# A decode step of attention and MLP: VectorE's keys in two steps of 24 blocks instead of four of 12

## The chip, the cores and the metric

One core of a Trainium2 chip runs the whole program. The metric is the device time of one execution in microseconds (us). A core has five engines that run their own instruction streams and meet only through semaphores: TensorE (PE, matmuls and transposes), VectorE (DVE), ScalarE (ACT), GpSimd (POOL) and SyncE (SP), which here issues nearly all DMAs. Data moves between device memory and the on-chip memory by DMA engines, and matmul results land in a second on-chip memory, PSUM.

## The reference

For one token `x` (512 values) the program computes two branches and mixes them by a gate. Branch A is attention over a cache of 4096 keys and values for each of 32 heads of 128 dimensions; branch B is an MLP with a squared ReLU.

```python
x = A_x
g = sigmoid((x * gate_w).sum(-1))
# A
q = (x @ wq)                                   # 32 heads x 128
scores = einsum("bhqd,bhkd->bhqk", q, k_cache) * 128 ** -0.5
o = einsum("bhqk,bhkd->bhqd", softmax(scores), v_cache)
a = o.reshape(1, 1, 4096) @ wo                 # 4096 -> 512
# B
h = x @ w1 + b1                                # 512 -> 1376
b = relu(h) ** 2 @ w2 + b2                     # 1376 -> 512
out = g * a + (1 - g) * b
```

The caches are 32 x 4096 x 128 in bf16, 33.6 MB each; with the weights 78.47 MB are read.

## The kernel before, in words

**Quads.** The heads are worked four at a time: a quad `q` (0 to 7) is four heads. A quad's keys are one load of 4 MiB (K0 to K7): partition `32 r + p` holds head `r`'s keys `128 p` to `128 p + 127`, one behind the other. The 128 keys of a partition are called blocks: block `b` is one key of each partition, 128 elements wide. Values are loaded likewise (V0 to V7; V7 in three parts). Two buffers are there for keys and two for values, so K of quad `q` can be loaded only when quad `q - 2` no longer needs its buffer.

**Scores on two engines.** The 128 blocks are shared out. 48 of them (`X_BLOCKS`, four runs of 12) go to VectorE: `ttr(q, j)` multiplies 12 blocks of keys by the query (`qb`, spread over the partitions) into `prod`, fp32 (L685), and sums each block's 128 products into one column of `S` (L689). The other 80 (`Y_BLOCKS`) go to TensorE, in ten groups of eight: `transposes` (L460), ScalarE copies them from PSUM (`evac`, L355), `scores` multiplies them by the query (L467), and ScalarE copies the result to `S` (`s_copy`, L361). `COLUMN` gives the column of `S` that a block has.

**Softmax and values.** VectorE's `smax(q)` takes the maximum of each partition (L694). TensorE turns the column of maxima into a row (`max_rows`, L488), VectorE takes the maximum of each head (`gmax`, L698 and L701), TensorE spreads it (`max_cols`, L492), and ScalarE computes the exponentials and their sums (`exps`, L372). `pv(q)` on TensorE sums the denominators (L497) and multiplies by the values (128 matmuls, L501). VectorE's `recip(q)` and `norm(q)` divide and multiply by the gate (L708, L716); `norm` signals `s_on`.

**Output.** For two quads at a time TensorE turns the normed outputs (`turn`, L519), spreads them (`spread`, L525) and multiplies by a quarter of `wo` (`out_rows`, L534; the loads are wo0 to wo3). The MLP's first layer (`mlp_h`, L509 and L513) runs once near the end, and the second (`mlp_out`, L545) last of all, from `w2a` (ten groups of 128 rows) and `w2b` (the 96 rows left over), loaded in five parts.

**TensorE's order** is a loop of turns written with branches; turn `t` works quads `2t` and `2t + 1`. In block `h1`, from turn 2 on, it takes one `s_on` and then runs `pv` of an odd quad; `turn` takes another `s_on`. Each taking waits for one `norm`, so the eight `norm` are taken in their order: `norm(0)` ahead of `pv(1)`, `norm(1)` in the next `turn`, `norm(2)` ahead of `pv(3)`, `norm(3)` in `turn`, `norm(4)` ahead of `pv(5)`, `norm(5)` in `turn`, `norm(6)` ahead of `pv(7)`, `norm(7)` in the last `turn`. Around them the order is: in turn 3 `pv(3)`, `max_rows(5)`, keys of quad 6, `max_cols(5)`, `turn`, `spread`, `pv(4)`, `out_rows`, `max_rows(6)`, keys of quad 7, `max_cols(6)`; in turn 4 `pv(5)`, `max_rows(7)`, `max_cols(7)`, `turn`, `spread`, `mlp_h`, `pv(6)`, `out_rows`; then `pv(7)`, `turn`, `spread`, `out_rows` and `mlp_out`.

**VectorE's order** is the loop at L733: for each quad four `ttr`, with small work in between: behind the first one `bias()` (in quad 1), behind the second `gmax` of the quad before, behind the third `recip` and `norm` of the quad three before (from quad 3 on), and `smax` at the end.

**SyncE's order** is `ORDER`: K0 K1 V0 K2 K3 V1 K4 V2 K5 V3 K6 V4 K7 V5 V6 V7, each load from quad 2 on behind a wait (`done`): for keys that VectorE (`s_sd`, L246) and TensorE's transposes (`s_t`, L247) are through with quad `q - 2`, for values that `pv(q - 2)` is (`s_pv`, L249). `w1` goes behind V0, wo0 behind K2, wo1 behind V4 and wo2 behind V5 (`WO_AT`), and wo3 and the parts of `w2` come at the end, the latter behind a wait for VectorE's last `ttr` (L275), since `prod` lies in the memory of `w2a` (L102). All go into one queue.

Of the kernel before, what the change touches and what calls it, by code (L numbers as in the profile page):

```python
# [5 lines left out]
def bass_gated_mix__gqa_block_cached__dense_activation_squared_relu__decode_kernel(  # L6
# [15 lines left out]
    fp32 = mybir.dt.float32  # L22
    bf16 = mybir.dt.bfloat16
# [6 lines left out]
    DM = 512  # L30
    F = 1376
    FG = 10
    FR = F - FG * 128
# [4 lines left out]
    R = 4  # L38
    NQ = NH // R
    NB = 128  # L40
    NP = 4
    PB = NB // NP
    XB = 12
    YB = PB - XB
    YQ = NP * YB
    GB = 8
    GQ = YQ // GB
    NS = 4
# [15 lines left out]
    QF = 4  # L64
    W2_PARTS = [(0, 4), (4, 8), (FG, FG + 1), (8, 9), (9, 10)]


    X_BLOCKS = [PB * j + b for j in range(NP) for b in range(XB)]
    Y_BLOCKS = [PB * j + b for j in range(NP) for b in range(XB, PB)]
    COLUMN = {b: c for c, b in enumerate(Y_BLOCKS + X_BLOCKS)}  # L70

    k_q = A_k_cache.rearrange("a (q r) (p b) d -> (a q) (r p) (b d)", r=R, p=32)
# [7 lines left out]
    with ctx:  # L80
        def sb(name, shape, dt):
            return ctx.enter_context(nc.sbuf_tensor(name, shape, dt))
# [4 lines left out]
        def sem(name):  # L87
            return ctx.enter_context(nc.semaphore(name))

        KV = sb("KV", [128, 4, NB * 128], bf16)  # L90
        W = sb("W", [128, 4 * 4096], bf16)
# [5 lines left out]
        sel0 = W[0:GH, 2 * TB * DM:2 * TB * DM + 2048]  # L97
        selB = sel0.rearrange("h (a c p) -> h a c p", a=2, c=8)
        w1_sb = sb("w1_sb", [128, 4, F], bf16)
        w2a = sb("w2a", [128, FG, DM], bf16)  # L100

        prod = w2a[:, :, :].rearrange("p g n -> p (g n)").bitcast(fp32)[:, 0:XB * 128]\  # L102
            .rearrange("p (b d) -> p b d", d=128)
        w2b = sb("w2b", [FR, DM], bf16)
        xcol = sb("xcol", [128, 4], bf16)
        xcolf = sb("xcolf", [128, 4], fp32)
        xrow = w1_sb[0:1, 0, 0:DM]
# [12 lines left out]
        qc2 = sb("qc2", [128, 2, R], bf16)  # L120
        S = sb("S", [128, NS, NB], fp32)
        E = sb("E", [128, 2, NB, R], bf16)
        mp = sb("mp", [128, 2], fp32)
# [69 lines left out]
        s_sd = sem("s_sd")  # L193
        s_pd = sem("s_pd")
# [23 lines left out]
        def key(q, b):  # L218
            return KV[:, K_SLOT[q], b * 128:(b + 1) * 128]

        def rows(r):
            return slice(32 * r, 32 * r + 32)
# [6 lines left out]
        @block.sync  # L229
        def _(eng):  # L230
            def load_kv(n):
                kind, q = ORDER[n]
                if q >= 2:
                    done(kind, q - 2)
                if kind == "K":
                    eng.dma_start(KV[:, K_SLOT[q], :], k_q[q, :, :]).then_inc(s_k[q], 16)
                else:
                    at = 0
                    for m, sv in zip(V_PARTS[q], s_v[q]):
                        a, b = at * PB * 128, (at + m) * PB * 128  # L240
                        eng.dma_start(KV[:, V_SLOT[q], a:b], v_q[q, :, a:b]).then_inc(sv, 16)  # L241
                        at += m

            def done(kind, q):
                if kind == "K":
                    eng.wait_ge(s_sd, NP * (q + 1))  # L246
                    eng.wait_ge(s_t, GQ * (q + 1))  # L247
                else:
                    eng.wait_ge(s_pv, q + 1)  # L249

            def load_wo(g):
                if g == 0:
                    eng.wait_ge(s_qps, NQ)
                elif g < NG - 1:
                    eng.wait_ge(s_wd, g)
                a = 0 if g < NG - 1 else 1
                eng.dma_start(wo_sb[:, a, :, :], wo_v[g, :, :, :]).then_inc(s_wo[a], 16)  # L257

            def load_w2(n):
                a, b = W2_PARTS[n]  # L260
                if a < FG:
                    eng.dma_start(w2a[:, a:b, :], w2_v[:, a:b, :]).then_inc(s_w2[n], 16)  # L262
                else:
                    eng.dma_start(w2b[:, :], B_w2[FG * 128:F, :]).then_inc(s_w2[n], 16)  # L264

            for n in range(len(ORDER)):
                load_kv(n)
                if n == 2:
                    eng.wait_ge(s_z, 1)
                    eng.wait_ge(s_b2, 1)  # L270
                    eng.dma_start(w1_sb[:, :, :], w1_v[:, :, :]).then_inc(s_w1, 16)
                if n in WO_AT:
                    load_wo(WO_AT[n])
            load_wo(NG - 1)
            eng.wait_ge(s_sd, NP * NQ)  # L275
            load_w2(0)
            load_w2(1)
            load_w2(2)
            load_w2(3)
            load_w2(4)  # L280
            eng.wait_ge(s_f4, 1)
            eng.dma_start(out[0, 0, :].rearrange("(j p) -> j p", p=128), fin4[:, :]).then_inc(s_out, 16)
# [38 lines left out]
        def _(eng):  # L321
# [35 lines left out]
            def s_copy(q):  # L357
                eng.wait_ge(s_s2, GQ * (q + 1))
                S2 = pS[:, 0:YQ * R].rearrange("p (b r) -> p b r", r=R)
                for r in range(R):  # L360
                    eng.activation(S[rows(r), q % NS, 0:YQ], S2[rows(r), :, r], ACT.Copy).then_inc(s_cp, 1)  # L361

# [45 lines left out]
        def _(eng):  # L408
# [48 lines left out]
            def transposes(a, g):  # L457
                for y in range(GB):
                    b = Y_BLOCKS[GB * g + y]
                    mm = eng.transpose(KP[(GQ * a + g) % NKP][:, y * 128:(y + 1) * 128], key(a, b), ident[:, :])  # L460
# [34 lines left out]
            def pv(a):  # L495
                take(s_e, R)
                eng.matmul(DEN[a], onesf[:, :], RS[:, a, :], start=True, stop=True)  # L497
                for j in range(NP):
                    take(s_vp)
                    for b in range(PB * j, PB * j + PB):  # L500
                        mm = eng.matmul(O[a], KV[:, V_SLOT[a], b * 128:(b + 1) * 128],  # L501
                                        E[:, a, COLUMN[b], :], start=(b == 0), stop=(b == NB - 1))
                mm.then_inc(s_pv, 1)
# [146 lines left out]
        def _(eng):  # L650
# [20 lines left out]
            def bias():  # L671
                eng.wait_ge(s_b2, 1)
                eng.tensor_scalar(b2g[:, :], B2, omg[:, 0:1], None, ALU.mult).then_inc(s_bg, 1)

            def ttr(q, j):
                if j == 0:
                    eng.wait_ge(s_k[q], 16)
                    eng.wait_ge(s_qb, R * (q + 1))
                    if q >= NS:
                        eng.wait_ge(s_pv, q - NS + 1)  # L680
                if q + j > 0:
                    eng.wait_ge(s_sd, NP * q + j)
                x = PB * j * 128
                c = COLUMN[PB * j]
                eng.tensor_tensor(prod, KV[:, K_SLOT[q], x:x + XB * 128].rearrange("p (b d) -> p b d", d=128),  # L685
                                  qb[:, q, :].unsqueeze(1).to_broadcast([128, XB, 128]), ALU.mult)\
                   .then_inc(s_pd, 1)
                eng.wait_ge(s_pd, NP * q + j + 1)
                eng.tensor_reduce(S[:, q % NS, c:c + XB], prod, AX.X, ALU.add).then_inc(s_sd, 1)  # L689

            def smax(q):
                eng.wait_ge(s_cp, R * (q + 1))
                eng.wait_ge(s_sd, NP * (q + 1))
                eng.tensor_reduce(mp[:, q % 2:q % 2 + 1], S[:, q % NS, :], AX.X, ALU.max).then_inc(s_mp, 1)  # L694

            def gmax(q):
                eng.wait_ge(s_mt, q + 1)
                eng.tensor_reduce(gm[:, q, :], MT.rearrange("o (r p) -> o r p", r=R), AX.X, ALU.max)\  # L698
                   .then_inc(s_gm, 1)
                eng.wait_ge(s_gm, q + 1)  # L700
                eng.tensor_scalar(dg[:, q % 2, :].rearrange("o (r p) -> o r p", r=R),  # L701
                                  gm[:, q, :].unsqueeze(2).to_broadcast([1, R, 32]), -SCALE, None, ALU.mult)\
                   .then_inc(s_dg, 1)

            def recip(q):
                a, b = R * q, R * q + R
                eng.wait_ge(s_pv, q + 1)
                eng.reciprocal(rden[:, a:b], DEN[q % 2]).then_inc(s_rd, 1)  # L708

            def norm(q):  # L710
                a, b = R * q, R * q + R
                eng.wait_ge(s_rd, q + 1)
                if q >= 2:

                    eng.wait_ge(s_ot, q // 2 * 2 - 1)
                eng.scalar_tensor_tensor(out=onorm[:, q % 2, :], in0=O[q % 2], scalar=gcol[:, 0:1],  # L716
                                         in1=rden[:, a:b], op0=ALU.mult, op1=ALU.mult)\
                   .then_inc(s_on, 1)
# [12 lines left out]
                                         op0=ALU.mult, op1=ALU.mult).then_inc(s_hs, 1)  # L731
            gate()
            for q in range(NQ):  # L733
                for j in range(NP):
                    ttr(q, j)
                    if j == 0 and q == 1:
                        bias()
                    if j == 1 and q >= 1:
                        gmax(q - 1)
                    if j == 2 and q >= 3:  # L740
                        recip(q - 3)
                        norm(q - 3)
                smax(q)
# [46 lines left out]
```

## Time and profile before

| what | value |
|---|---|
| three runs, median | 190.8 us (190.54 to 190.84) |
| the profiled execution | 190.55 us, span 189.2 us |
| PE busy | 137.1 us (72%) |
| VectorE busy | 123.0 us (65%) in 123 instructions |
| ScalarE busy | 116.0 us (61%) |
| read from device memory | 78.32 MB, 414 GB/s over the span |
| DMA queue 1, share of 16 engines | 97.1% |
| VectorE, products (L685) | 32 of 128 x 1536, mean 1760 ns, 56.3 us |
| VectorE, sums (L689) | 32 of 128 x 1536, mean 1753 ns, 56.1 us |
| VectorE idle before L685, for keys | 19.0 us in six waits |
| mean granted TensorE clock | 0.735 |

The profile is one execution, and its span runs from the first to the last instruction; what lies around it, 190.55 less 189.2, is 1.35 us. Busy time is counted by engine; DMA issues and waits are not busy. In a timeline a line gives the start and the duration in us, the engine, the line of the kernel, the operation, what it writes and reads, and in brackets how long its engine was idle before and what ended that. "SPq" is the queue of SyncE's DMA issues, "PEq" TensorE's sequencer, and "issue" time in which no releaser is seen.

### The profile page before, as it was taken

How to read it: one execution, taken by the hardware profiler on the slowest of the kernel's cores; microseconds unless marked ns; L12 is line 12 of the kernel's file. 1: busy time of each engine (PE TensorE's matmuls, PEld its weight loads, DVE VectorE, ACT ScalarE, POOL GpSimd, SP SyncE). 2: the span in 40 equal slices, each digit the busy share in tenths (PEclk: the TensorE clock that was granted, in tenths of full speed). 3: DMA queues.
4: the chain of work that ended last, by engine and by line, in shares of the span. 5: the costliest groups of instructions: out<-in, count | busy, mean ns of one | idle time of the engine just before them, and what ended most of it. 6: DMA issues, size and time to landing. Idle time of an engine off the chain costs nothing. (4 is left out here: it accounts for less than half of the span.)

```text
span 189.2 us, 6234 instructions
## 1 busy us (share of the span) xinstructions
PE 137.1 (72%) x2688; PEld 119.8 (63%) x2688; DVE 123.0 (65%) x123; ACT 116.0 (61%) x243; POOL 6.0 (3%) x13
## 2 busy tenths in 40 slices
PE   0009297668849979969968797829868496889865
PEld 0003165537739779758958696829767495879864
DVE  0110099979969999996998299919990499701010
ACT  3004559948989986984987099708973298560000
POOL 4000000000700000000000000000000000000000
PEclk9999969958975975995795559655985579555555
DMA  6999999989989999999999999999999999999992
GB/s 225 437 444 443 443 443 426 443 361 483 440 360 436 443 443 440 417 436 430 443 424 409 423 443 443 436 436 436 414 445 409 416 443 443 438 388 416 421 388 78
DMA packets 4177, 78.47 MB, mean 415 GB/s; under 512 B 483, under 2 KB 837, under 8 KB 1094
## 3 DMA queue, kind: packets, MB, share of 16 engines
q1 hardware_dynamic: 4152, 78.32, 97.1%
q8 instruction: 7, 0.11, 0.2%
q14 instruction: 4, 0.03, 0.0%
q10 hardware_dynamic: 14, 0.01, 0.0%
HBM read 78.32 MB, written 0.00 MB: 414 GB/s over the span
## 5 line engine op out<-in xcount | busy, mean ns | idle before, releaser
L355 ACT ACTIVATE kT<-KP 128x1024 bf16<-128x1024 bf16 x80 | 75.3, 1041 | 26.1 <-PE KP L460 25.9
L685 DVE TENSOR_TENSOR w2a<-KV,qb 128x1536 f32<-128x1536 bf16 x32 | 56.3, 1760 | 19.4 <-DMA KV<-in_A_k_cache_dram 19.0
L460 PE MATMUL KP<-ident,KV 128*128 128x128 bf16 x640 | 59.6, 256 | 10.5 <-PEq L455 10.5
L460 PEld LDWEIGHTS KP<-ident,KV 128*128 128x128 bf16 x640 | 48.4, 116 | 14.1 <-issue 13.1
L689 DVE TENSOR_REDUCE S<-w2a 128x12 f32<-128x1536 f32 x32 | 56.1, 1753 | 1.1
L467 PE MATMUL pS<-qc,kT 128*128 128x4 bf16 x640 | 28.1, 166 | 13.0 <-PEq L455 11.0
L467 PEld LDWEIGHTS pS<-qc,kT 128*128 128x128 bf16 x640 | 24.6, 99 | 18.9 <-issue 17.6
L501 PEld LDWEIGHTS pO<-E,KV 128*128 128x128 bf16 x1024 | 29.3, 105 | 0.0
L501 PE MATMUL pO<-E,KV 128*128 128x4 bf16 x1024 | 28.4, 166 | 0.0
L372 ACT ACTIVATE E<-S,nM 32x128 bf16<-32x128 f32 x32 | 18.5, 578 | 0.9
L445 PE MATMUL pQ<-W,xb 128*128 128x512 bf16 x20 | 7.8, 532 | 7.2 <-DMA W<-in_A_wq_dram 6.1
L338 ACT ACTIVATE qb<-pQ 32x128 bf16<-32x128 f32 x20 | 5.4, 268 | 9.7 <-PE pQ L445 9.3
L361 ACT ACTIVATE S<-pS 32x80 f32<-32x80 f32 x32 | 7.3, 228 | 4.8 <-PE pS L467 4.2
L445 PEld LDWEIGHTS pQ<-W,xb 128*128 128x128 bf16 x20 | 2.2, 126 | 9.6 <-DMA W<-in_A_wq_dram 6.2
L372 ACT ACTIVATION_READ_ACCUMULATOR E<-S,nM 32x1 f32 x32 | 8.1, 252 | 0.0
L664 DVE TENSOR_SCALAR e<-ez 128x1 f32<-128x1 f32 x1 | 0.2, 153 | 10.8 <-ACT ez L387 10.8
L708 DVE RECIPROCAL rden<-pO 128x4 f32<-128x4 f32 x8 | 1.4, 174 | 8.2 <-PE pO L501 8.2
L594 PE MATMUL pO<-ident,w_sb 1*128 1x1 bf16 x4 | 0.3, 165 | 7.8 <-DMA w_sb<-in_A_x_dram 7.8
L497 PE MATMUL pO<-RS,onesf 128*128 128x4 f32 x16 | 4.3, 339 | 1.8 <-PEq L455 1.8
L655 DVE TENSOR_SCALAR xb<-zeros,xcolf 128x128 bf16<-128x128 bf16 x4 | 0.7, 248 | 7.5 <-ACT xcolf L331 7.5
L488 PE MATMUL pM<-identf,mp 128*1 128x128 f32 x8 | 3.0, 372 | 3.4 <-PEq L455 3.1
L497 PEld LDWEIGHTS pO<-RS,onesf 128*128 128x128 f32 x16 | 3.8, 298 | 2.1 <-issue 2.0
(75 smaller groups left out, 72.2 us busy)
## 6 DMA issues: line engine op xcount, KB each, us to landing
KV<-in_A_k_cache_dram SPq DMA_DIRECT2D x8, 4096.0 KB, 22.0
KV<-in_A_v_cache_dram SPq DMA_DIRECT2D x7, 4096.0 KB, 29.5
W<-in_A_wq_dram SPq DMA_DIRECT2D x1, 4096.0 KB, 13.4
W<-in_A_wo_dram SPq DMA_DIRECT2D x4, 1024.0 KB, 16.5
KV<-in_A_v_cache_dram SPq DMA_DIRECT2D x1, 2048.0 KB, 11.0
KV<-in_A_v_cache_dram SPq DMA_DIRECT2D x2, 1024.0 KB, 14.1
w_sb<-in_B_w_dram SPq DMA_DIRECT2D x1, 1376.0 KB, 24.4
w2a<-in_B_w_dram SPq DMA_DIRECT2D x2, 512.0 KB, 18.5
```

Of the source, the lines that this page charges most:

```text
L338: eng.activation(qb[rows(r), c, :], QR[c][rows(r), r * 128:(r + 1) * 128], ACT.Copy)\
L355: eng.activation(kT[:, n % NT, :], KP[n % NKP][:, :], ACT.Copy).then_inc(s_ev, 1)
L361: eng.activation(S[rows(r), q % NS, 0:YQ], S2[rows(r), :, r], ACT.Copy).then_inc(s_cp, 1)
L372: eng.activation(E[rows(r), q % 2, :, r], S[rows(r), q % NS, :], ACT.Exp, bias=nM[rows(r), q:q + 1], scale=SCALE, accum_out=RS[rows(r), q ...
L445: mm = eng.matmul(QR[c], xb[:, t, :], wq_sb[:, t, c * 512:(c + 1) * 512], start=(t == 0), stop=(t == 3))
L460: mm = eng.transpose(KP[(GQ * a + g) % NKP][:, y * 128:(y + 1) * 128], key(a, b), ident[:, :])
L467: mm = eng.matmul(pS[:, R * c:R * c + R], kT[:, (GQ * a + g) % NT, y * 128:(y + 1) * 128], qc2[:, a, :], start=True, stop=True)
L488: eng.transpose(MT, mp[:, a:a + 1], identf[:, :]).then_inc(s_mt, 1)
L497: eng.matmul(DEN[a], onesf[:, :], RS[:, a, :], start=True, stop=True)
L501: mm = eng.matmul(O[a], KV[:, V_SLOT[a], b * 128:(b + 1) * 128], E[:, a, COLUMN[b], :], start=(b == 0), stop=(b == NB - 1))
L685: eng.tensor_tensor(prod, KV[:, K_SLOT[q], x:x + XB * 128].rearrange("p (b d) -> p b d", d=128), qb[:, q, :].unsqueeze(1).to_broadcast([12 ...
L689: eng.tensor_reduce(S[:, q % NS, c:c + XB], prod, AX.X, ALU.add).then_inc(s_sd, 1)
```

## The change

A quad's first 48 blocks are VectorE's, in one run, instead of four runs of 12; they are worked in `NX` = 2 steps of `XB` = 24 blocks. The counts in the waits on `s_sd` and `s_pd` follow (`NX` for `NP`). `prod` grows from 12 to 24 blocks, 12 KiB a partition; it lies in a new buffer `w2x` of `FG + 2` rows of 512, of which `w2a` is the first ten and `w2b` row ten. In VectorE's loop `gmax` goes behind the first of two steps, and `recip` and `norm` behind the second.

```diff
-    XB = 12
-    YB = PB - XB
-    YQ = NP * YB
+    NX = 2
+    XB = 24
+    YQ = NB - NX * XB
...
-    X_BLOCKS = [PB * j + b for j in range(NP) for b in range(XB)]
-    Y_BLOCKS = [PB * j + b for j in range(NP) for b in range(XB, PB)]
+    X_BLOCKS = list(range(NX * XB))
+    Y_BLOCKS = list(range(NX * XB, NB))
...
-        w2a = sb("w2a", [128, FG, DM], bf16)
-        prod = w2a[:, :, :].rearrange("p g n -> p (g n)").bitcast(fp32)[:, 0:XB * 128]\
+        w2x = sb("w2x", [128, FG + 2, DM], bf16)
+        w2a = w2x[:, 0:FG, :]
+        w2b = w2x[0:FR, FG, :]
+        prod = w2x[:, :, :].rearrange("p g n -> p (g n)").bitcast(fp32)[:, 0:XB * 128]\
             .rearrange("p (b d) -> p b d", d=128)
-        w2b = sb("w2b", [FR, DM], bf16)
...
-                    eng.wait_ge(s_sd, NP * (q + 1))
+                    eng.wait_ge(s_sd, NX * (q + 1))
...
-                    eng.wait_ge(s_sd, NP * q + j)
-                x = PB * j * 128
-                c = COLUMN[PB * j]
+                    eng.wait_ge(s_sd, NX * q + j)
+                x = XB * j * 128
+                c = COLUMN[XB * j]
...
-                for j in range(NP):
+                for j in range(NX):
                     ttr(q, j)
                     if j == 0 and q == 1:
                         bias()
-                    if j == 1 and q >= 1:
+                    if j == 0 and q >= 1:
                         gmax(q - 1)
-                    if j == 2 and q >= 3:
+                    if j == 1 and q >= 3:
                         recip(q - 3)
                         norm(q - 3)
                 smax(q)
```

The waits on `s_sd` ahead of the `w2` loads, on `s_pd` in `ttr` and on `s_sd` in `smax` change from `NP` to `NX` in the same way.

More of the change, by code (lines that the diff above doesn't have):

```diff
@@ L274, in _ @@
             load_wo(NG - 1)
-            eng.wait_ge(s_sd, NP * NQ)
+            eng.wait_ge(s_sd, NX * NQ)
             load_w2(0)
@@ L687, in ttr @@
                    .then_inc(s_pd, 1)
-                eng.wait_ge(s_pd, NP * q + j + 1)
+                eng.wait_ge(s_pd, NX * q + j + 1)
                 eng.tensor_reduce(S[:, q % NS, c:c + XB], prod, AX.X, ALU.add).then_inc(s_sd, 1)
@@ L692, in smax @@
                 eng.wait_ge(s_cp, R * (q + 1))
-                eng.wait_ge(s_sd, NP * (q + 1))
+                eng.wait_ge(s_sd, NX * (q + 1))
                 eng.tensor_reduce(mp[:, q % 2:q % 2 + 1], S[:, q % NS, :], AX.X, ALU.max).then_inc(s_mp, 1)
```

## The prediction

> **What bounds the kernel now.** I read the page's slices first, then the chain of waits that ended last, then SyncE's own timeline, and last the timelines of the engines from the landing of the last keys to the end.
>
> The slices, GB/s and busy tenths of the DMA engines:
>
> ```profile
> DMA  6999999989989999999999999999999999999992
> GB/s 225 437 444 443 443 443 426 443 361 483 440 360 436 443 443 440 417 436 430 443 424 409 423 443 443 436 436 436 414 445 409 416 443 443 438 388 416 421 388 78
> ```
>
> The DMA engines are full nearly throughout; queue 1 holds them 97.1% of the span. The chain of waits ends the same way:
>
> ```profile
> 168.56 18.33 DMA w2a<-in_B_w_dram
> ...
> 186.94 0.28 PE pQ L545 x4
> ```
>
> The last part of `w2` lands at 186.9 us, 18.33 us after its issue, because it stands behind everything issued earlier. So the first limit is the transfer stream, and VectorE sets it only where a load is issued too late. VectorE releases the K slots at L246 (SyncE waits there 26.4 us in six waits). K7 is issued at 122.55 us, with K6 (starts VectorE at 127.13), V4 and wo1 still ahead of it: it lands at about 148.9. The stream has several us in hand at each issue, so an earlier release of a K slot moves no byte.
>
> The second limit is close behind. This is the timeline of the last 29 us, all engines:
>
> ```profile
> 160.06 0.38 PE L492 MATMUL pM<-onesf,dg 1*128 1x1 f32 x2
> 160.19 0.22 DVE L716 SCALAR_TENSOR_TENSOR onorm<-pO,gcol,rden 128x4 bf16<-128x4 f32 x1
> 160.87 0.56 PE L497 MATMUL pO<-RS,onesf 128*128 128x4 f32 x2 [0.43 <-PEq L455]
> ...
> 164.87 1.28 SPq L241 DMA_DIRECT2D KV<-in_A_v_cache_dram  x3
> ...
> 182.25 0.22 DVE L716 SCALAR_TENSOR_TENSOR onorm<-pO,gcol,rden 128x4 bf16<-128x4 f32 x1
> ...
> 182.62 0.27 PE L519 MATMUL KP<-ident,onorm 128*8 128x128 bf16 x1 [0.62 <-PEq L455]
> ...
> 184.35 0.99 PE L534 MATMUL pQ<-o,W 128*128 128x1 bf16 x32 [0.50 <-PEq L455]
> ...
> 186.06 0.58 PE L545 MATMUL pQ<-hs,w2a 128*128 128x1 bf16 x16 [0.29 <-DMA w2a<-in_B_w_dram]
> ```
>
> TensorE works without a long pause from `pv(5)` (160.87) through `max_rows(7)`, `turn`, `spread`, `mlp_h`, `pv(6)`, `out_rows(0)`, `pv(7)` and `out_rows(1)` to the `w2` products at 185.20, and only there waits for data. How much in hand: 44 products of `w2` at 27.5 ns each (128 of L501 take 3.55 us) would follow on each other from 185.20, the last four starting at 185.20 + 40 x 0.0275 + two or three handoffs of 0.02 = 186.34. They start at 186.94. TensorE has 0.60 us of slack against the stream, no more.
>
> The reader is to see the second and third line: `pv(5)` starts 0.46 us behind the end of `norm(4)` (160.19 + 0.22 = 160.41). It is no accident: in the block `h1` TensorE takes `s_on`, the signal of `norm(4)`, ahead of `pv(5)`.
>
> **The change part by part.** VectorE's part of the last quad, now:
>
> ```profile
> 149.06 1.76 DVE L685 TENSOR_TENSOR w2a<-KV,qb 128x1536 f32<-128x1536 bf16 x1 [6.72 <-DMA KV<-in_A_k_cache_dram]
> 150.85 1.75 DVE L689 TENSOR_REDUCE S<-w2a 128x12 f32<-128x1536 f32 x1
> 152.63 1.76 DVE L685 TENSOR_TENSOR w2a<-KV,qb 128x1536 f32<-128x1536 bf16 x1
> 154.43 1.75 DVE L689 TENSOR_REDUCE S<-w2a 128x12 f32<-128x1536 f32 x1
> 156.10 0.27 DVE L698 TENSOR_REDUCE gm<-pM 1x4 f32<-1x128 f32 x1
> ...
> 156.54 1.74 DVE L685 TENSOR_TENSOR w2a<-KV,qb 128x1536 f32<-128x1536 bf16 x1
> 158.32 1.75 DVE L689 TENSOR_REDUCE S<-w2a 128x12 f32<-128x1536 f32 x1
> 159.99 0.17 DVE L708 RECIPROCAL rden<-pO 128x4 f32<-128x4 f32 x1
> ```
>
> *Removed and added.* 64 instructions of 1536 elements become 32 of 3072. Their price is in no row. From the reduce of L694 (128 elements, 0.28 us) to that of L689 (1536, 1.753) the slope is 1.473 / 1408 = 1.046 ns an element, so a reduce of 3072 is 1.753 + 1.607 = 3.36; the product, 1.757 against L756's 0.16 at 4 elements, gives 1.757 + 1.601 = 3.36 too. I take 3.36. From above, two old ones on end, 3.51; from below, 0.946 ns an element (if 0.3 us of the old one were fixed), 3.21. A step is 2 x (3.36 + 0.03) = 6.78, against 7.16 for two old pairs: 0.38 saved, 0.76 a quad, 6 us over eight quads. All of it lies beside the stream: worth nothing at the end.
>
> [...]
>
> *Moved.* `gmax(q-1)` stays behind 24 blocks. The move that counts: `recip(q-3)` and `norm(q-3)` stood behind 36 of the 48 blocks and now stand behind all 48, just ahead of `smax(q)`. In the last quad, whose start is K7's landing and stays at 149.06: a step 6.78, `gmax` 0.32 (156.54 - 154.43 - 1.79), a step 6.78, less 0.12, as `recip` starts 1.67 behind the reduce and not 1.79: `recip` at 162.82, `norm` ends 0.42 later, 163.24. That is 2.83 behind 160.41.
>
> *Who waits.* TensorE's `take(s_on)`, and queued behind it `pv(5)` and all the rest of its program. From `norm`'s end to its first dependent product 0.15 us pass (182.47 to 182.62); I take 0.2 for the taking of `s_e` as well: `pv(5)` at 163.45, **2.58 late** (163.39 to 163.7 from the two gaps, 0.15 and 0.46). Behind it nothing absorbs this: `max_rows(7)` needs `smax(7)`, which comes earlier (163.5 for 164.25) but was not awaited; `gmax(7)`, `norm(5)`, ACT's copies and `exps(7)` follow from TensorE's own steps; V6 has landed (about 170.7: 148.9, then V5, wo2 and V6, 9.44 MB at 431 GB/s); V7 has landed by about 180.5, ahead of `pv(7)` at 180.6 to 184.6. So `out_rows(1)` at 186.9, the `w2` products 187.8 to 189.2, no longer waiting for the stream.
>
> *SyncE's queue.* V7 waits for `pv(5)` (L249): issue 164.87 becomes 167.45, and wo3 and the five parts of `w2` behind it shift as much, the last from 168.56 to 171.1. The stream has V6 to move until 170.7, so it does not run dry: 3.2 us in hand, where it had 5.8.
>
> *The same wait one quad earlier.* `norm(0)` to `norm(3)` gate `pv(1)`, `turn`, `pv(3)`, `turn` likewise, 1 to 2.6 us late each. Quad 6 as the example: `norm(3)` ends at 127.13 + 14.18 = 141.31 and not 138.50, `turn` at 141.46 and not 138.96; ACT's copy behind it was held 0.35 us by other work and is so no longer, so `max_rows(6)` comes 2.2 later, 147.7 for 145.50. Keys(7) starts at K7's landing all the same: there TensorE idles 3.35 us now (3.44 before K6), and the V slots come free ahead of the stream. So these cost nothing; without that idle time keys(7) would start up to 2.2 late, and pv(5) with it where it is not held longer by `norm`.
>
> *Nothing else.* Which 48 blocks VectorE takes changes no transfer; `w2b` in `w2x` was already loaded behind the last reduce; `bias()` comes behind 24 blocks of quad 1 and not 12, so at 39.73 + 6.78 = 46.5 and not 43.2; `zero`, which needs it, runs at 51.75.
>
> **Sum.** 2.58 late, less 0.60 of slack: +1.98. On the profiled execution (span 189.2, time 190.55) that is a span of 191.2 and 192.5; its time lies 0.25 under the median of 190.8, so 192.5 to 192.8. I say **192.7 us**, 1.0% slower. Instructions of 3.21 to 3.51 move `norm` by 0.6 either way, the handoff by 0.25: 191.9 to 193.5 for this case.
>
> **Rivals.**
> 1. *Hidden by the stream* (190.8): `norm(4)` would have to end by 161.0, which needs steps of 5.7 instead of 6.78. The slopes of both rows speak against it. Chance 0.05.
> 2. *Faster* (190.4): the K slots are freed 0.4 to 0.8 us earlier, and slices 8 and 11 (361 and 360 GB/s) show low rates about where K2 and K3 are issued (38.28, 54.63). If the stream starved there, the earlier issue would fill it. Price: the loads between the starts of VectorE on K0 and K2 (23.97, 56.61) are 13.99 MB, 32.4 us at the steady 432 GB/s (8.39 MB from 88.29 to 107.71, the starts on K4 and K5) against 32.64, and from K2 to K4 31.55 against 31.68: 0.4 us at most. It decides only if the wait on `norm` costs under 0.2 net. Slice 9's 483 speaks for records that end late rather than a dry queue. Chance 0.06.
> 3. *Slower still* (about 194): V7's later issue lets the queue run dry, or the delay of quad 6 reaches keys(7). The first needs 3.2 us more than I have and then moves V7's landing by the gap; the second has 148.9 - 147.7 = 1.2 us in hand. One us beyond its margin gives 193.7, somewhat more 194. Chance 0.11.
>
> **The numbers.** Forecast 0.78, rivals 0.05, 0.06, 0.11. A difference under 0.2% (0.4 us) is about what a measurement of this kernel can't tell from none. Slower 0.88, same 0.06, faster 0.06. The range, 191.4 to 193.7, leaves the first two and the top of the third out.
>
> **What would show it.** 16 products and 16 reduces at 3.3 to 3.4 us; in the last quad `norm(4)` ending near 163.2; `pv(5)` starting right behind it, with TensorE idle about 2.6 us before; the `w2` products without waits for their data, so that the chain of waits runs through TensorE and VectorE's L716 and no longer through the DMA of `w2`; GB/s as before up to 165 us. It is wrong if `pv(5)` starts by 161.5, if the chain still ends in the landing of `w2`, or if a gap shows in the stream before 184.

## The result, and the profile after

The changed kernel takes 192.47 us (median of four runs, 192.37 to 192.62) against 190.8 before (190.54 to 190.84): 0.9% slower, ratio 1.0091 with a 95% interval of 1.0074 to 1.0108. The profiled execution took 192.37 us, its span is 191.0: 1.8 us more than the profiled execution before.

First the groups of VectorE's products and sums (count, busy us, mean ns, idle time before them): one line from the page of the kernel before, then the two of the changed kernel, whose lines stand two further down (L687 is the L685 of before):

```profile
L685 DVE TENSOR_TENSOR w2a<-KV,qb 128x1536 f32<-128x1536 bf16 x32 | 56.3, 1760 | 19.4 <-DMA KV<-in_A_k_cache_dram 19.0
...
L687 DVE TENSOR_TENSOR w2x<-KV,qb 128x3072 f32<-128x3072 bf16 x16 | 53.6, 3349 | 22.2 <-DMA KV<-in_A_k_cache_dram 22.1
L691 DVE TENSOR_REDUCE S<-w2x 128x24 f32<-128x3072 f32 x16 | 53.7, 3353 | 0.6
```

32 instructions of 3.35 us stand where 64 of 1.76 stood: VectorE works 107.3 us on them and not 112.4. The idle time before L687 has grown from 19.4 to 22.2 us: more than half of the 5 us saved in work is VectorE waiting longer for keys. The keys come when they did, within 0.2 us. The starts of the last quad in the changed kernel's timeline of VectorE, and what follows:

```profile
148.90 3.36 DVE L687 TENSOR_TENSOR w2x<-KV,qb 128x3072 f32<-128x3072 bf16 x1 [7.54 <-DMA KV<-in_A_k_cache_dram]
152.30 3.35 DVE L691 TENSOR_REDUCE S<-w2x 128x24 f32<-128x3072 f32 x1
155.57 0.27 DVE L700 TENSOR_REDUCE gm<-pM 1x4 f32<-1x128 f32 x1
...
156.01 3.34 DVE L687 TENSOR_TENSOR w2x<-KV,qb 128x3072 f32<-128x3072 bf16 x1
159.39 3.35 DVE L691 TENSOR_REDUCE S<-w2x 128x24 f32<-128x3072 f32 x1
162.66 0.17 DVE L710 RECIPROCAL rden<-pO 128x4 f32<-128x4 f32 x1
162.86 0.22 DVE L718 SCALAR_TENSOR_TENSOR onorm<-pO,gcol,rden 128x4 bf16<-128x4 f32 x1
163.00 0.28 DVE L696 TENSOR_REDUCE mp<-S 128x1 f32<-128x128 f32 x1
```

`norm(4)` (L718) ends at 163.08; before, it ended at 160.41. `smax(7)` (L696) comes at 163.00 and not 163.97, which helps nobody. The same stretch and the end on TensorE (the number in brackets is its idle time):

```profile
159.87 0.58 PE L494 MATMUL pM<-onesf,dg 1*128 1x1 f32 x2
163.38 0.56 PE L499 MATMUL pO<-RS,onesf 128*128 128x4 f32 x2 [2.93 <-PEq L457]
...
186.87 0.99 PE L536 MATMUL pQ<-o,W 128*128 128x1 bf16 x32 [0.50 <-PEq L457]
187.72 1.31 PE L547 MATMUL pQ<-hs,w2x 128*128 128x1 bf16 x44
```

`max_cols(6)` (L494) is over at 160.45, and `pv(5)` (L499) starts at 163.38, 0.30 behind the end of `norm(4)`: 2.93 us idle where there were 0.43. The 44 products of `w2` (L547) now run as one piece: none waits for its data. So the chain of waits that ended last has changed its kind:

```profile
186.87 0.99 PE pQ L536 x32
187.86 1.19 PE pQ L547 x44
189.05 0.02 issue
189.07 0.17 DVE accs L758
```

It is TensorE's own work, and no longer 18.33 us of `w2`'s transfer. The view breaks off at 186.83, so it does not itself reach back to `norm(4)`; the experiments have to show that link.

### The profile page after: what moved, and what is told of

It is laid out like the page before. It is cut to its first block, busy times and chain, and to the rows that moved or that the text cites. A ratio compares the mean times of both kernels' runs of the same rounds, so it can differ in the third digit from the quotient of the medians.

```text
span 191.0 us, 6199 instructions
## 1 busy us (share of the span) xinstructions
PE 136.6 (72%) x2685; PEld 119.4 (63%) x2688; DVE 117.9 (62%) x91; ACT 115.9 (61%) x243; POOL 6.9 (4%) x13
## 5 line engine op out<-in xcount | busy, mean ns | idle before, releaser
L687 DVE TENSOR_TENSOR w2x<-KV,qb 128x3072 f32<-128x3072 bf16 x16 | 53.6, 3349 | 22.2 <-DMA KV<-in_A_k_cache_dram 22.1
L462 PE MATMUL KP<-ident,KV 128*128 128x128 bf16 x640 | 58.5, 252 | 3.6 <-PEq L457 3.6
L691 DVE TENSOR_REDUCE S<-w2x 128x24 f32<-128x3072 f32 x16 | 53.7, 3353 | 0.6
L462 PEld LDWEIGHTS KP<-ident,KV 128*128 128x128 bf16 x640 | 47.6, 115 | 6.9 <-issue 5.7
L469 PEld LDWEIGHTS pS<-qc,kT 128*128 128x128 bf16 x640 | 24.1, 99 | 19.7 <-issue 18.1
L447 PE MATMUL pQ<-W,xb 128*128 128x512 bf16 x17 | 6.7, 528 | 7.7 <-DMA W<-in_A_wq_dram 6.4
L499 PE MATMUL pO<-RS,onesf 128*128 128x4 f32 x16 | 4.5, 352 | 6.5 <-PEq L457 6.5
L499 PEld LDWEIGHTS pO<-RS,onesf 128*128 128x128 f32 x16 | 4.0, 313 | 6.7 <-issue 6.7
L380 ACT ACTIVATE oT<-KP 8x128 bf16<-8x128 bf16 x3 | 0.8, 266 | 9.3 <-PE KP L521 9.3
```

The source lines that it names most:

```text
L447: mm = eng.matmul(QR[c], xb[:, t, :], wq_sb[:, t, c * 512:(c + 1) * 512], start=(t == 0), stop=(t == 3))
L469: mm = eng.matmul(pS[:, R * c:R * c + R], kT[:, (GQ * a + g) % NT, y * 128:(y + 1) * 128], qc2[:, a, :], start=True, stop=True)
```

## The experiments

The theory: the end moves because `pv(5)` waits for `norm(4)`, which the change put behind all 48 blocks of quad 7, less what TensorE had in hand. The rivals: the large steps or the new buffer cost by themselves; the delays of quads 3 to 6 add up; each missed place costs a fixed step; the later issue of V7 and `w2`, which follows from the later `pv(5)`, is what costs.

**Recip and norm behind the first step.** In the changed kernel:

```diff
-                    if j == 1 and q >= 3:
+                    if j == 0 and q >= 3:
                         recip(q - 3)
                         norm(q - 3)
```

> The changed kernel, with recip and norm behind the first of the two steps and not the second. Theory (TensorE waits for norm(4) ahead of pv(5)): norm(4) ends near 156.6, pv(5) starts behind max_cols(6) near 160.7, as before the change, and the time goes back to 190.5 to 190.9. Rival (the large steps or the new buffer cost by themselves): stays at 192.2 to 192.6. Rival (the time before was itself held by norm): below 190.4.

Measured: 190.74 us, as much as the kernel before beside it (190.74; ratio 0.9995, 0.9986 to 1.0004). VectorE and TensorE in this kernel's timelines, and the end of its chain of waits:

```profile
156.34 0.22 DVE L718 SCALAR_TENSOR_TENSOR onorm<-pO,gcol,rden 128x4 bf16<-128x4 f32 x1
```

```profile
160.16 0.38 PE L494 MATMUL pM<-onesf,dg 1*128 1x1 f32 x2
160.97 0.56 PE L499 MATMUL pO<-RS,onesf 128*128 128x4 f32 x2 [0.43 <-PEq L457]
```

```profile
168.66 18.18 DMA w2x<-in_B_w_dram
...
186.89 0.28 PE pQ L547 x4
```

`norm(4)` is done at 156.56, `pv(5)` starts 0.43 behind `max_cols(6)` as it did before the change, and the chain ends again in the landing of `w2`. With `recip` and `norm` behind the first step, the large steps and the new buffer cost nothing. They gain nothing either, though `norm` is 3.9 us earlier than in the kernel before: that kernel was not held by it.

**Behind the first step in quad 7 alone.** The change's place stays for quads 3 to 6:

```diff
-                    if j == 1 and q >= 3:
+                    if q >= 3 and j == (0 if q == NQ - 1 else 1):
```

> The changed kernel, with recip and norm behind the first step in quad 7 alone; quads 3 to 6 stay as the change has them. Theory: only norm(4) is paid for, the delays of turn and pv in quads 3 to 6 end in TensorE's idle time before the next keys: 190.5 to 190.9. Rival (the delays of the earlier quads add up): about halfway, 191.3 to 192.0.

Measured: 190.69 us (0.9997, 0.9988 to 1.0006). **And its complement**, late in quad 7 alone:

```diff
-                    if j == 1 and q >= 3:
+                    if q >= 3 and j == (1 if q == NQ - 1 else 0):
```

> The complement of norm_first_q7_only: recip and norm behind the second step in quad 7 alone, behind the first in quads 3 to 6. Theory: the whole cost is there, 192.3 to 192.7. Rival (the earlier quads pay part): 191.2 to 192.0.

Measured: 192.51 us (1.0091, 1.0076 to 1.0107), the changed kernel's time. The two together: the whole cost is paid at one place out of five, quad 7. TensorE waits at the others too (1.10, 1.67, 1.92 and 2.72 us idle in the changed kernel ahead of `pv(1)`, `turn`, `pv(3)` and `turn`), and nothing comes of it. TensorE's timeline around quad 6, in the kernel before and in the changed one:

```profile
145.50 0.37 PE L488 MATMUL pM<-identf,mp 128*1 128x128 f32 x1
149.22 2.72 PE L460 MATMUL KP<-ident,KV 128*128 128x128 bf16 x24 [3.35 <-PEq L455]
```

```profile
141.32 0.27 PE L521 MATMUL KP<-ident,onorm 128*8 128x128 bf16 x1 [2.72 <-PEq L457]
...
147.59 0.37 PE L490 MATMUL pM<-identf,mp 128*1 128x128 f32 x1
149.06 2.72 PE L462 MATMUL KP<-ident,KV 128*128 128x128 bf16 x24 [1.10 <-PEq L457]
```

In the changed kernel `turn` (L521) waits 2.72 us for `norm(3)`, `max_rows(6)` (L490) is 2.1 later than before, and the keys of quad 7 start with K7's landing all the same, behind 1.10 us of idle time that were 3.35.

**The place alone, in the kernel before.** Steps of 12, blocks and buffers as they were:

```diff
-                    if j == 2 and q >= 3:
+                    if j == 3 and q >= 3:
                         recip(q - 3)
                         norm(q - 3)
```

> The kernel before, with recip and norm behind the fourth step of 12 blocks and not the third; steps, blocks and buffers as before. Theory: norm(4) ends 3.58 later, at 164.0, pv(5) starts 0.14 behind it, 3.3 late; less 0.60 of slack +2.7: 193.4 to 193.6. Rival (the large steps or the layout cost, not the place of norm): 190.7 to 190.9.

Measured: 193.34 us (1.0133, 1.0118 to 1.0149), just under what was expected. VectorE and TensorE in its timelines:

```profile
163.84 0.22 DVE L716 SCALAR_TENSOR_TENSOR onorm<-pO,gcol,rden 128x4 bf16<-128x4 f32 x1
```

```profile
164.36 0.56 PE L497 MATMUL pO<-RS,onesf 128*128 128x4 f32 x2 [3.69 <-PEq L455]
```

**Half as late**, between the product and the reduce of the fourth step:

```diff
             def ttr(q, j):
...
+                if j == 3 and q >= 3:
+                    recip(q - 3)
+                    norm(q - 3)
                 eng.wait_ge(s_pd, NP * q + j + 1)
...
-                    if j == 2 and q >= 3:
-                        recip(q - 3)
-                        norm(q - 3)
```

> The kernel before, with recip and norm between the product and the reduce of the fourth step of 12 blocks. Theory (the end moves by the lateness of pv(5) less a fixed slack): norm(4) ends 1.79 later, at 162.2, pv(5) starts at 162.35, 1.5 late; less 0.60 of slack +0.9: 191.5 to 191.8. If the slack is 0.8, as the spacing of the later cases suggests: 191.4. Rival (there is a step, a missed place costs 1.7 or more whatever its lateness): 192.2 or more.

Measured: 191.41 us (1.0039, 1.0025 to 1.0053), under the 191.5 that a slack of 0.60 was to give and at what 0.8 gives. No large step is in either kernel, and the cost is there, growing with the lateness and not as one jump.

**The other half of the change alone**: the run of 48 blocks and the shared buffer, with steps of 12.

```diff
-    NX = 2
-    XB = 24
+    NX = 4
+    XB = 12
...
-                    if j == 0 and q >= 1:
+                    if j == 1 and q >= 1:
                         gmax(q - 1)
-                    if j == 1 and q >= 3:
+                    if j == 2 and q >= 3:
```

> The changed kernel's run of 48 blocks and its shared buffer, but four steps of 12 and gmax, recip and norm behind the steps where the kernel before has them. Theory: nothing, 190.6 to 191.0. Rival (contiguous blocks or the place of w2 cost): 191.5 or more.

Measured: 190.82 us against 190.86 beside it (1.0003, 0.9988 to 1.0018). Nothing.

**Two more places in the changed kernel.** Between the product and the reduce of the second step:

```diff
             def ttr(q, j):
...
+                if j == 1 and q >= 3:
+                    recip(q - 3)
+                    norm(q - 3)
                 eng.wait_ge(s_pd, NX * q + j + 1)
...
-                    if j == 1 and q >= 3:
-                        recip(q - 3)
-                        norm(q - 3)
```

> The changed kernel, with recip and norm between the product and the reduce of the second step, that is near 159.7 for norm(4), 0.7 ahead of where it ended before the change. Theory: pv(5) no longer waits for it (max_cols(6) ends near 160.4), 190.5 to 190.9. Rival (large steps or buffer): 192.2 to 192.6.

Measured: 190.79 us (0.9989, 0.9976 to 1.0002). And behind `smax`:

```diff
-                    if j == 1 and q >= 3:
-                        recip(q - 3)
-                        norm(q - 3)
                 smax(q)
+                if q >= 3:
+                    recip(q - 3)
+                    norm(q - 3)
```

> The changed kernel, with recip and norm behind smax and not ahead of it. Theory: norm(4) ends 0.2 to 0.4 later than in the changed kernel, and since no slack is left the end moves by as much: 192.65 to 192.9. Rival (the end is held by something else, so that norm has slack): 192.4 to 192.5.

Measured: 192.80 us (1.0103, 1.0088 to 1.0118). `norm(4)` ends at 163.59 there, 0.51 later than in the changed kernel; 0.12 of that is a later landing of K7 (149.02 for 148.90), so 0.39 is the move itself, within what was put. The time is 0.33 longer.

All the kernels that differ in the place of `norm` or in the layout, in the order in which `norm(4)` ends in the profiled executions. K7's landing varies by up to 0.5 us between them (VectorE starts on it at 148.89 to 149.38) and moves `pv(5)` with it:

| kernel | norm(4) ends | pv(5) starts | span | time, median |
|---|---|---|---|---|
| changed, norm behind the first step | 156.56 | 160.97 | 189.1 | 190.74 |
| changed, the same in quad 7 alone | 156.91 | 161.32 | 189.5 | 190.69 |
| changed, norm inside the second step | 159.69 | 160.83 | 189.5 | 190.79 |
| changed layout, steps of 12 | 160.27 | 160.84 | 189.4 | 190.82 |
| before | 160.41 | 160.87 | 189.2 | 190.8 |
| before, norm inside the fourth step | 162.07 | 162.37 | 190.1 | 191.41 |
| changed | 163.08 | 163.38 | 191.0 | 192.47 |
| changed, norm late in quad 7 alone | 163.21 | 163.51 | 191.1 | 192.51 |
| changed, norm behind smax | 163.59 | 163.89 | 191.6 | 192.80 |
| before, norm behind the fourth step | 164.06 | 164.36 | 192.0 | 193.34 |

Up to 160.41, the latest of the first five, the place of `norm` is free. From 162.07 on `pv(5)` starts 0.30 after it in all five kernels, and the span grows by 1.9 us for 1.99 of `pv(5)` (162.37 to 164.36). Counted from 160.87 and 189.2, the lateness not paid for is 1.50 - 0.9 = 0.6, 2.51 - 1.8 = 0.7 and 3.49 - 2.8 = 0.7 us: a fixed slack, then one for one. Steps of 12 and of 24 lie on one line. Counted by the medians, each against the kernel before beside it, the same lateness leaves 0.8 to 1.1 us unpaid, mostly because the profiled execution of the kernel before is 0.25 faster than its median.

**V7 issued late, all else as before.** In the kernel before, SyncE holds V7 until `spread` of turn 4:

```diff
                 else:
                     eng.wait_ge(s_pv, q + 1)
+                    if q == NQ - 3:
+                        eng.wait_ge(s_ot, 2 * NG - 2)
```

> The kernel before, with SyncE's issue of V7 held until the spread of turn 4, near 167.6, and wo3 and the parts of w2 behind it; TensorE and VectorE as before. Theory: the stream still has V6 until 170.7, so the time stays at 190.6 to 191.0. Rival (the later issues of V7 and w2 that came with the change are what costs): 192.0 to 192.8.

Measured: 191.22 us against 190.74 beside it (1.002, 1.0007 to 1.0033). That is neither the forecast of no change nor the rival's 1.3 and more: +0.5. The profiled execution is one of its faster ones, 190.94 us, 0.39 over the profiled one before. Two lines of this kernel's chain of waits, the issue of V7 and the end of the transfers:

```profile
167.71 0.33 SPq L241
...
172.49 14.80 DMA w2a<-in_B_w_dram
```

V7 is issued at 167.71, in the changed kernel at 167.39. The last part of `w2` lands at 172.49 + 14.80 = 187.29, 0.39 behind the kernel before (186.90). Where the stream loses it shows in a window from 168 to 172 us (busy us and instruction counts of the engines, granted clock, DMA share, GB/s), in the kernel before, with V7 late, and in the changed kernel:

```profile
168.00:172.00 4.00, 4.00 (x45) 3.78 (x44) 0.00 (x0) 2.21 (x8) 0.00 (x0) 0.50 0.90 381
```

```profile
168.00:172.00 4.00, 4.00 (x44) 3.76 (x44) 0.00 (x0) 2.29 (x8) 0.00 (x0) 0.50 0.88 336
```

```profile
168.00:172.00 4.00, 3.25 (x41) 2.98 (x42) 0.47 (x3) 2.07 (x9) 0.00 (x0) 0.50 0.85 336
```

45 GB/s less for 4 us is 0.18 MB, 0.4 us at the 426 GB/s that the kernel before moves from 166 to 170 us. The first five kernels of the table, which issue V7 at 164.77 to 165.10, move 377 to 397 GB/s in this window, the two that issue it at 167.39 and 167.71 move 336. So the late issue of V7, and of `wo3` and `w2` queued behind it, did cost the stream about 0.4 us.

The transfers' own records show where part of it goes. From 168.5 to 170 us the kernel before has 16.1 packets of queue 1 under way on average and never fewer than 16. In the changed kernel it is 14.1 on average and 12 at the least, although V6 lands only at 170.99. The landing is signalled in 16 parts, of which the first comes at 168.87: some of V6 was through 2.1 us ahead of its last part. That the missing packets belong to the parts already through is not shown, since the records do not tell which part a packet is of. By their number, 2.0 of 16 for 1.5 us, the missing packets are worth an estimated 0.19 us, about half of the 0.4 us, and the other half stays open.

In the changed kernel the end does not show this: the last part of `w2` is issued at 171.4 and takes 16.1 us, so it lands at 187.5, and TensorE's last four products come at 187.72 + 40 x 0.0275 = 188.8. It is hidden behind the wait that caused it.

## Why the prediction was right

- **What bounds the kernel: right.** The stream, with TensorE 0.60 us behind it. The table gives 0.6 to 0.7 by the spans, 0.8 to 1.1 by the medians.
- **The price of a step: right.** 3.36 us an instruction from the slopes of the two rows; 3.35 measured, for both (means 3349 ns for the product, 3353 for the sum). Two old ones took 2 x 1760 and 2 x 1753 ns, so a large one takes 0.17 and 0.15 us less than two of them.
- **VectorE's saving is worth nothing: right**, shown by the first experiment: the large steps with `norm` behind the first one run in the time of the kernel before.
- **The moved step: right**, in place and size. `recip` was put at 162.82 and came at 162.66, with K7 0.16 earlier; `norm`'s end at 163.24, came at 163.08.
- **Who waits: right.** `pv(5)` was put at 163.45 and started at 163.38. The handoff took 0.30 and not 0.2, and K7's earlier landing made up for it, which was luck.
- **Nothing absorbs it: right.** From the start of `pv(5)` to `out_rows(1)` it is 23.48 us before (160.87 to 184.35) and 23.49 after (163.38 to 186.87).
- **The earlier quads cost nothing: right**, shown by quad 7 late alone and early alone. The margin before keys(7) was put at 1.2 us; TensorE idles 1.10.
- **SyncE's queue: wrong.** "It does not run dry: 3.2 us in hand" counted the bytes of V6 up to its landing; from 168.5 to 170 us 14.1 packets were under way on average, where the kernel before has 16.1. With the same late issue and nothing else the stream loses 0.4 us. In the changed kernel it moves 131 GB/s from 168 to 169 us, where the kernel before moves 295: that is a dip of the kind that the prediction named as a sign of being wrong. V7's last part lands at 181.2 and not by 180.5, when `pv(7)` has begun (180.55); `pv(7)` takes that part last and does not wait. None of this changed the sum, because TensorE was later still; had the slack been larger than the lateness, it would have been the whole effect.
- **The chain: half seen.** It no longer ends in the landing of `w2`, as forecast, but the view does not reach back to L716. That `norm(4)` sets the end is shown by the table instead.
- **The sum.** +1.98 forecast, +1.82 between the two profiled executions (190.55 and 192.37), +1.67 between the medians. The term that is too large is the end of TensorE's chain: the last product ends at 189.05 and not 187.22 + 1.98 = 189.20. 0.07 of that is `pv(5)`'s start, and the rest lies in the 44 products, which take 1.33 us from the first start to the last end where I had 1.42 with two or three handoffs in between. What remains to the medians is how far each profiled execution lies from its own median: 0.25 before, 0.10 after.

Of the rivals, "hidden by the stream" would have needed a slack four times as large (its limit for `norm(4)`, 161.0, is a little low: the prediction's own 160.87 + 0.60 - 0.2 is 161.27). "Faster" did not come. The K slots are freed earlier, K7 is issued at 121.42 and not 122.55, and slice 11, which that rival named, moves 412 GB/s for 360. But K7's start on VectorE, 148.90 for 149.06, is no earlier than in the kernel with the changed layout and the old steps (148.91), and in other executions of kernels with large steps it was 149.04 and 149.38.

## What to carry to other kernels

An instruction loop is also a timetable: when steps get longer and fewer, there are fewer points between them for small work, and it moves by up to a step. Before merging steps, list each small instruction between them, who waits for it, and how long before its need it is done now: here `norm` ended 0.46 us ahead of `pv(5)`, of which the handoff takes 0.30, and the move was 2.7. Place such work by its consumer's need and not by the step number nearest to the old one: behind the first step it was free, and so it was between the product and the sum of the second.

## What the runs showed that I had not expected

A transfer queue that by bytes still had some 3 us of work (V7 issued at 167.39 and V6 landed at 170.99 in the changed kernel) moved 336 GB/s instead of 377 to 397 in the window from 168 to 172: packets were missing from the queue some 2.5 us ahead of V6's landing. With V7 late alone, at 167.71, the rate was the same and the last landing came 0.39 us later. And two instructions of VectorE, `recip` and `norm`, of 0.17 and 0.22 us, set 0.9% of the whole time by their place in one quad alone, while 32 instructions less on the same engine, 5 us of work, set none of it.
